# A linear-attention and gated-convolution kernel: nine tokens of a head on a partition, and K and Q transposed by DMA

## The chip, the cores and the metric

The kernel runs on one core of one Trainium2 chip. A core has a matrix engine (TensorE, "PE" in the profile, its weight loads "PEld"), three engines for elementwise work (VectorE "DVE", ScalarE "ACT", GpSimd "POOL"), a queue that only issues DMAs (SyncE, "SP") and 16 DMA engines. TensorE reads SBUF, the on-chip memory of 128 partitions, and writes PSUM, here eight banks of 128 x 512 fp32 values. Each engine runs its own instructions in order and waits for others by semaphores. The metric is the device time of one execution in microseconds, less is better.

## The reference

There are 8 batches of 8 heads, 576 tokens, head size 64, and 128 features. The first half is linear attention, and its output, heads side by side (512 wide), goes through a gated causal convolution:

```python
def phi(x):
    proj = np.einsum('bhsd,df->bhsf', x, w_phi)
    proj = proj - np.max(np.abs(proj), axis=-1, keepdims=True)
    return np.concatenate([np.exp(proj), np.exp(-proj)], axis=-1)
q_p, k_p = (phi(q), phi(k))
kv = np.einsum('bhsf,bhsd->bhfd', k_p, v)
z = np.sum(k_p, axis=2)
num = np.einsum('bhsf,bhfd->bhsd', q_p, kv)
den = np.einsum('bhsf,bhf->bhs', q_p, z)[..., None] + 1e-06
x = num / den                       # heads side by side: (8, 576, 512)

for k in range(5):                  # xp: x with four zero rows ahead
    gate_pre += conv_w[k][None, None, :] * xp[:, k:k + S, :]
gate = 1.0 / (1.0 + np.exp(-gate_pre))
out = gate * (x @ w_val) @ w_out
```

The inputs and the output are fp32; the kernel multiplies in bf16.

## The kernel before

**Tiling of the attention.** The first 512 tokens of a head lie four consecutive ones to a partition on 128 partitions (`main_src`, line 179: `j=4`). The last 64 tokens of the heads are the "tails": those of two batches share 128 partitions, 64 rows each. A *unit* is 1024 rows of K and of Q, eight blocks of 128 rows by 64 values: a main unit is a pair of heads, a tail unit the tails of all 16 heads of two batches. So there are 32 main and 4 tail units, numbered 0 to 35, a tail unit first in each group of nine.

Each unit goes through the same steps. `T` (line 331): eight TensorE transposes of 128x128, two blocks each, four of K and four of Q, into one PSUM bank. `Tc`: one copy to the SBUF tile `T`, by DVE (`D`) or ScalarE (`A`). `PK` and `PQA` (line 342): projections of K and Q with tokens on partitions, 16 matmuls each that use 64 rows of the array, two row halves in turn. `mKa`, `mK`, `mQa`, `mQ` (line 356): the largest absolute value of a row, on DVE. `K0` to `K3` (line 388): exponentials of K's projection, on ScalarE. `E` (line 382): exponentials of the row maximum, which go onto V rather than K. `V` (line 408): V times that factor, mostly on POOL, with the factor itself as a 65th column so that the sum `z` comes along. `PQ` and `SH` (lines 466, 476): Q's projection with features on partitions, and the subtraction of its row maximum by matmuls with a negated identity. `Qa`, `Q` (line 484): its exponentials.

`KV` (lines 445, 450): for a head pair, 16 matmuls with the main blocks and 4 with the tails, 65 columns each; the tails' V tile (`VZ`) is zero in the other batch's rows, so the contraction runs over all 128. `KVM`: the copy to SBUF. `NUM`: 16 matmuls per main unit (line 509), and per tail unit 32 that use half of the array's columns (line 523). `XN` (lines 534, 536): reciprocal and multiplication. `XP` (lines 545, 548): a DMA transpose of the result, issued by SP, into `XT` (main) or `XH` (tails).

**The second half.** `GA` (line 604): the convolution as matmuls with diagonal 64x64 weights, on the four quarters of the array, per batch in two ops. The tokens of a partition differ by their offset j = 0 to 3, so a tap is a shift of j, and where it crosses the four a shift by one partition. `VAa`, `VAb` (line 617): x times `w_val`. `TH`: tanh for the gate. `GV` (line 633): gate times value. `OUT` (line 642): times `w_out`; `OE` the copy out with a factor 0.5, `ST` the store by SP. `GAt`, `THt`, `GVt`, `OUTt`, `OEt` and `STt` do the same for the tails, and `HL` copies the four tokens ahead of a tail.

**What sets the order.** The string `ORDER` (lines 32 to 101) lists every step in turn, with PSUM banks after `@` and the engine after `:`. Each engine gets its instructions in that order, and the DMAs their queue: loads of fp32 inputs, cast to bf16 on the way, are issued by POOL (`LD`, line 295; V of batch 0 by SP, uncast), transposes and stores by SP. Tile pools give the buffers: five of `T`, three of `VT`, thirteen of `KVS`.

Of the kernel before, what the change touches and what calls it, by code (L numbers as in the profile page):

```python
# [42 lines left out]
SH7 mQa8 LD15 mK8 K08 K37 PQA9@2,3 mQ8 mQa9 KV5@7 KVM5:D mQ9 T10@5 Tc10:D K18 PQ8@0,2 SH8 Qa7
PK9@4,7 mKa9 T11@3 E7 V7:P Q7 PK10@5,6 Tc11:D K28 mKa10 LD14 DG0:P Qa8 K38 KV6@3 Q8 K09 NUM5@0 mK9
KVM6:D NUM6@2 XN5 K010 mK10 KV7@0 K29 K110 XN6 K19 KVM7:D T12@5 PK11@1,4 mKa11 K210 HL0:P Tc12:D
XP6 LD16 K39 GA0@2 K310 mK11 K011 NUM7@6 VAa1@0 LD40 XN7 E8 VAb1 TH0 GV1 V8:P PK12@2,5 PQA10@3,6
K111 PQ9@1,7 SH9 VAa2@0 K211 mQa10 mKa12 LD19 VAa0@3 mK12 E9 LD17 K311 Qa9 VAb0 mQ10 KV8@4 KVM8:D
VAb2 GV0 PQA11@1,6 K012 V9:P Q9 mQa11 K212 PQ10@4,7 SH10 mQ11 K112 T13@3 Tc13:D NUM8@1 XN8 E10
K312 Qa10 Q10 GA1@5 TH1 PK13@3,4 mKa13 NUM0@1 V10:P KV10@7 XN0 KVM10:D XP5 XP0 XP8 E11 E12 K013
mK13 VAa3@5 GV2 PQ11@6,1 SH11 K113 Qa11 V11:P VAb3 GV3 LD18 K213 NUM10@2 XN10 T14@0 Tc14:D Q11  # L50
KV11@7 XP7 PQA12@5,6 K313 GA2@2 E13 TH2 PK14@0,1 mQa12 mQ12 PQA14@4,5 OUT1@6 OE1:A KVM11:D
PQA13@7,2 mQa14 V12:P V13:P mKa14 LD34 K014 mQ14 mQa13 K114 PQ12@3,4 SH12 XP10 KV12@6 mQ13 T15@5
Qa12 KVM12:A Tc15:D OUT2@7 Q12 mK14 K214 NUM11@2 E14 PQ13@0,6 SH13 Qa13 XN11 XP11 NUM12@4 OE2:D
XN12 T16@2 VAa6@3 PK15@7,0 mKa15 GA3@4 mK15 K314 V14:P VAa4@1 Q13 Tc16:D VAb4 K015 TH3 PQA15@6,2
GV4 K215 K315 PQ14@5,4 SH14 mQa15 K115 mQ15 VAa5@1 VAb5 PK16@0,6 Qa14 VAb6 Q14 KV13@7 GV5 mKa16
mK16 Vb9:P K016 VAa7@2 T17@1 GV6 E15 V15:P Tc17:D LD33 KVM13:A KV14@5 LD22 HL1:P NUM13@3 K116 K216
PQ15@0,7 KVM14:A VAb7 XN13 K316 SH15 GV7 PK17@1,3 mKa17 Qa15 K017 Q15 K117 LD35 mK17 XP13
PQA16@5,6 mQa16 OUT3@4 XP12 K217 OE3:D mQ16 OUT0@2 OUT5@0 K317 OE5:A E16 V16:P OE0:D NUM14@4 T18@1
XN14 Tc18:D GAt0@6 THt0 ST1 GVt0 E17 PQ16@2,3 PK18@1,0 SH16 Qa16 mKa18 Q16 T19@4 Tc19:D GA4@5 TH4
PQA18@7,2 mK18 mQa18 E18 KV15@4 KVM15:D K018 LD38 K118 V17:P K218 OUT6@3 mQ18 OE6:D PQA17@7,6 K318  # L60
mQa17 mQ17 LD20 GA5@4 TH5 PK19@2,3 mKa19 PQ18@1,7 SH18 K019 KV16@0 mK19 Qa18 KVM16:D K119 E19
NUM15@5 VAa9@4 VAb9 LD21 V19:P K219 ST3 XN15 XP15 GV9 NUM16@0 XN16 Q18 LD24 T20@2 VAa8@5 XP16 VAb8
K319 T21@6 PQA19@4,0 PQ17@1,7 Tc20:D PK20@2,3 Tc21:A SH17 GV8 Qa17 mQa19 VAa10@5 VAb10 mKa20 K020
XP14 KV17@6 V18:P mQ19 Q17 GV10 VAa11@0 PK21@1,4 KVM17:D K120 mK20 mKa21 mK21 K220 VAb11 GV11
NUM17@5 XN17 OUTt0@2 K021 K221 LD26 KV19@7 OUT7@0 K320 OEt0:D OE7:D K121 T22@3 PQA20@5,2 mQa20
PQ19@1,6 mQ20 SH19 KVM19:A K321 Tc22:A HL2:A PK22@0,5 mKa22 NUM9@3 XN9 XP9 Qa19 OUT4@7 Q19 K022
E20 mK22 Vb18:P PQA21@2,1 mQa21 XP17 OE4:D K122 K222 T23@6 K322 V20:P E21 NUM19@3 XN19 XP19 E22
PQ20@2,0 V21:P SH20 Qa20 mQ21 OUT9@7 OE9:D LD23 PQA22@5,4 mQa22 Tc23:D Q20 LD36 mQ22 PQ21@3,1 SH21
KV20@7 KVM20:A LD25 Qa21 V22:P T24@2 PQA23@6,0 mQa23 PK23@5,7 mKa23 Q21 OUT8@4 OE8:A K023 OUT10@3
mK23 E23 V23:P OUT11@6 Tc24:D OE10:D NUM20@1 K223 K323 K123 XN20 XP20 OE11:A GA6@3 PK24@1,2  # L70
PQ22@7,5 SH22 ST5 T25@6 TH6 mKa24 mK24 Tc25:D Qa22 Q22 E24 K024 KV21@3 KVM21:D KV22@4 GA7@6
KVM22:D HL3:D mQ23 NUM21@4 TH7 VAa14@3 XN21 XP21 VAb14 K124 NUM22@6 LD37 K224 PQA24@1,5 GV14
PQ23@0,4 SH23 K324 Qa23 XN22 PK25@3,6 Q23 mQa24 mKa25 K025 KV23@7 T26@2 Tc26:A V24:P VAa15@1
KVM23:D VAb15 mQ24 ST7 K125 NUM23@4 mK25 K225 VAa12@0 VAb12 GV15 XN23 PK26@2,1 PQ24@7,3 K325
PQA25@4,5 mKa26 K026 E25 mQa25 SH24 Qa24 GV12 VAa13@6 mQ25 VAb13 T27@4 KV24@0 mK26 K126 Q24 XP23
PQ25@5,7 SH25 GV13 Tc27:D T28@2 Qa25 Q25 E26 KVM24:D Tc28:D XP22 PQA26@6,3 mQa26 mQ26 OUT13@4
V25:P V26:P K226 PK27@0,2 mKa27 LD28 OE13:A GAt1@5 mK27 KV25@7 K326 THt1 GVt1 K027 NUM24@3 K127
E27 K227 Vb27:P KVM25:D XN24 KV26@1 PK28@5,6 mKa28 XP24 LD27 K327 PQ26@7,0 SH26 mK28 Qa26 NUM25@3
XN25 HL4:A OUTt1@2 Q26 K028 K128 KVM26:D OUT14@7 OE14:D XP25 K228 PQA27@3,4 mQa27 mQ27 GA8@0 TH8
VAa16@7 VAb16 K328 OEt1:A NUM26@4 XN26 T29@3 Tc29:A NUM18@0 XN18 XP18 E28 OUT12@6 V28:P PK29@3,2  # L80
GV16 OE12:A PQ27@5,4 mKa29 PQA28@0,1 mQa28 mQ28 K029 SH27 Qa27 GA9@6 TH9 T30@0 ST11 VAa18@1 mK29
VAb18 Tc30:D PK30@0,5 GV18 V27:P OUT15@6 VAa17@7 VAb17 mKa30 Q27 OE15:D mK30 K129 E29 PQA29@4,6
V29:P mQa29 GV17 mQ29 PQ28@1,3 K229 K030 K130 SH28 T31@0 Tc31:D K230 VAa19@4 VAb19 Qa28 KV28@7 ST9
XP26 K329 PQA30@6,1 PQ29@2,0 SH29 GV19 mQa30 mQ30 Q28 KVM28:A K330 NUM28@3 XN28 PQ30@7,6 Qa29 E30
V30:P PK31@5,1 mKa31 SH30 PQA31@4,3 Q29 Qa30 mQa31 mK31 E31 mQ31 KV29@2 V31:P K031 K231 T32@0
OUT17@4 Tc32:D K131 OUT16@7 Q30 PK32@0,3 KVM29:D OE17:D KV30@2 mKa32 K331 OE16:A NUM29@4 KVM30:D
K032 T33@6 XP28 mK32 XN29 XP29 GA10@1 LD29 K132 Tc33:D PQA32@4,5 K232 K332 E32 PQ31@7,0 mQa32
HL5:P TH10 mQ32 OUT19@6 OE19:A NUM30@3 XN30 XP30 KV31@5 KVM31:A SH31 Qa31 Q31 PQA33@1,6 PK33@2,3
ST15 mKa33 mQa33 mQ33 GA11@4 VAa20@7 TH11 VAb20 VAa22@1 mK33 V32:P VAb22 T34@6 PQ32@4,5 K033 SH32
E33 GV22 Tc34:D NUM31@0 VAa21@6 VAb21 GV20 K133 XN31 V33:P PK34@2,7 K233 K333 mKa34 Qa32 Q32 mK34  # L90
XP31 PQ33@3,4 K034 K134 T35@0 STt1 KV32@1 KVM32:D OUT18@5 NUM32@1 K234 K334 ST13 SH33 GV21 VAa23@6
VAb23 OE18:A Tc35:D PK35@7,0 XN32 XP32 Qa33 Q33 GV23 mKa35 PQA34@5,1 mQa34 mQ34 K035 GAt2@2 THt2
VAa26@6 E34 mK35 GVt2 ST17 V34:P VAb26 K135 KV33@4 PQA35@5,1 E35 mQa35 PQ34@7,2 SH34 VAa27@3 K235
K335 Qa34 mQ35 Q34 VAb27 STt0 KVM33:D PQ35@1,0 GA13@4 TH13 V35:D GV26 SH35 OUT20@7 KV34@2 Qa35
OE20:A KVM34:A VAa25@4 Q35 OUT21@5 NUM33@1 XN33 NUM34@6 KV35@0 VAb25 XP33 XN34 OE21:A KVM35:A
VAa24@5 OUT22@2 HL6:D XP34 OE22:D ST19 NUM35@0 VAb24 XN35 GA12@6 XP35 TH12 GV24 GA14@0 GV25 ST21
OUT23@2 GV27 VAa29@6 TH14 VAb29 HL7:D VAa31@7 VAb31 OUTt2@4 GV29 VAa28@3 NUM27@0 XN27 XP27 GA15@5
OEt2:A VAa30@4 OUT26@0 OUT27@1 OE26:D TH15 OUT24@6 OE24:D OUT25@5 VAb28 VAb30 STt2 GV31 OE23:A
OE27:D GAt3@6 GV30 GV28 OE25:A THt3 GVt3 OUT29@5 OUT28@0 ST23 OE29:A OUTt3@7 OE28:A OUT31@0
OUT30@1 OEt3:A ST27 ST25 ST29 OE31:A ST28 STt3 ST31 OE30:D ST30  # L100
"""


class _U:
    pass

@with_exitstack
def kernel(  # L110
# [653 lines left out]
```

## Time and profile before

| | before |
|---|---|
| time, median of 3 runs | 233.53 us (233.13 to 233.78) |
| profiled execution | 234.24 us, of it span 232.5 us |
| mean granted TensorE clock | 0.972 |
| busy: TensorE, ScalarE, DVE, POOL | 205.8, 188.6, 184.2, 125.4 us |
| HBM read, written | 30.48 MB, 9.44 MB |
| DMA packets | 62002, of them 33420 under 512 bytes |

The span is the time from the first to the last instruction of the program on the core; the profiled execution has 1.74 us around it. The busy time of an engine is the union of its instructions' times; those of TensorE are pipelined, so that a matmul of 200 ns can start 30 ns after the one before it. What a group of matmuls costs is therefore read from one group's start to the next one's. In rows of the profile `x16` is a count, `128x65` partitions by elements, and `64*128` the rows and columns of the array that are used. Brackets or a last column tell how long the engine sat idle before, and what ended it.

### The profile page before, as it was taken

To read this page: it belongs to the slowest core of one execution; us is meant where nothing else is said; L and a number is where in the kernel's file an instruction comes from. 1 tells how busy PE (TensorE), PEld (TensorE's weight loads), DVE (VectorE), ACT (ScalarE), POOL (GpSimd) and SP (SyncE) were. 2 spreads that over 40 slices of the span, in tenths; PEclk is the share of its full clock that TensorE was granted. 3 is DMA by queue.
4 is the path that set the end of the run, shared out by engine and by line. 5 is a ranking of instruction groups with operands and counts; after the bars stand their busy time and mean duration, and the time that the engine had idled before them with its cause. 6 is when DMAs were issued, how large, how long until landed. Compare 5 with 4: busy or idle time off the path is not lost.

```text
span 232.5 us, 8372 instructions
## 1 busy us (share of the span) xinstructions
PE 205.8 (89%) x3497; PEld 139.5 (60%) x3516; DVE 184.2 (79%) x335; ACT 188.6 (81%) x419; POOL 125.4 (54%) x142
## 2 busy tenths in 40 slices
PE   1286797888999989899999999999899999999991
PEld 1264675666666746567666766766476667564550
DVE  5559669999989979699999879897799788554451
ACT  3189869999997988599999979998899999934251
POOL 8909935999979437774919751564526241100000
PEclk9998579999999999999999999999999999999997
DMA  8997995979999942999994992499903928126195
GB/s 151 246 198 97 106 180 80 92 101 178 129 194 128 139 32 32 129 257 177 128 114 68 180 186 92 39 115 126 214 6 37 169 77 259 38 52 200 27 355 185
DMA packets 62002, 30.90 MB, mean 133 GB/s; under 512 B 33420, under 2 KB 59148, under 8 KB 61964
## 3 DMA queue, kind: packets, MB, share of 16 engines
q0 software_dynamic: 36144, 14.29, 58.2%
q1 hardware_dynamic: 25468, 15.78, 33.6%
q8 instruction: 27, 0.44, 0.8%
q10 hardware_dynamic: 352, 0.30, 0.4%
q14 instruction: 11, 0.09, 0.2%
HBM read 30.48 MB, written 9.44 MB: 172 GB/s over the span
## 4 chain that ended last, share of the span: by engine, by line
PE 69%; ACT 11%; DMA 9%; DVE 5%; issue 3%; SPq 1%; POOL 1%; POOLq 0%; DVEq 0%; ACTq 0%
PE PS L617 11%; PE PS L642 10%; PE PS L342 7%; PE PS L604 7%; PE PS L476 7%; PE PS L445 6%; PE PS L331 6%; DMA XT<-XN 6%; PE PS L509 5%; ACT QTIL L484 5%; ACT KTIL L388 3%; DMA kT<-in_k_dram 3%; PE PS L466 3%; PE PS L681 2%; DVE MQ L356 2%
## 5 line engine op out<-in xcount | busy, mean ns | idle before, releaser
L408 POOL TENSOR_TENSOR VT<-vN,E 128x1024 bf16<-128x1024 bf16 x27 | 51.5, 1907 | 60.4 <-issue 34.2
L388 ACT ACTIVATE KTIL<-PS 128x512 bf16<-128x512 f32 x128 | 76.7, 666 | 5.3 <-DVE MK L356 5.1
L484 ACT ACTIVATE QTIL<-PS 128x512 bf16<-128x512 f32 x128 | 71.0, 666 | 2.5 <-PE PS L476 1.1
L356 DVE TENSOR_REDUCE MK<-PS 128x4 f32<-128x512 f32 x72 | 47.9, 683 | 7.5 <-PE PS L342 7.2
L356 DVE TENSOR_REDUCE MQ<-PS 128x4 bf16<-128x512 f32 x72 | 47.4, 683 | 1.3 <-PE PS L342 1.2
L342 PE MATMUL PS<-W,T 64*128 64x128 bf16 x576 | 29.6, 227 | 5.8 <-DVE T L224 1.9
L617 PE MATMUL PS<-XT,WVAL 128*128 128x512 bf16 x128 | 33.8, 380 | 0.3 <-DMA XT<-XN 0.3
L342 PEld LDWEIGHTS <-T 64*128 64x128 bf16 x576 | 18.3, 98 | 21.8 <-issue 11.9
L642 PE MATMUL PS<-WOUT,GV 128*128 128x512 bf16 x111 | 29.9, 380 | 1.2 <-issue 0.5
L633 DVE SCALAR_TENSOR_TENSOR GV<-GATE,PS 128x512 bf16<-128x512 bf16 x32 | 21.6, 681 | 5.9 <-ACT GATE L612 3.1
L445 PE MATMUL PS<-VT,KTIL 128*128 128x65 bf16 x512 | 25.4, 198 | 0.8 <-DVE T L224 0.6
L536 DVE TENSOR_TENSOR XN<-PS,RCP 128x512 bf16<-128x512 f32 x36 | 24.9, 691 | 1.2
L445 PEld LDWEIGHTS <-KTIL 128*128 128x128 bf16 x512 | 22.8, 100 | 3.7 <-DVE T L224 0.8
L476 PE MATMUL PS<-nident,MQ 128*128 128x128 bf16 x288 | 23.9, 229 | 0.5 <-issue 0.5
L612 ACT ACTIVATE GATE<-PS 128x1024 bf16<-128x1024 f32 x16 | 16.7, 1044 | 8.8 <-PE PS L604 8.7
L476 PEld LDWEIGHTS <-MQ 128*128 128x128 bf16 x288 | 17.6, 102 | 9.5 <-issue 8.8
L224 DVE COPY T<-PS 128x1024 bf16<-128x1024 bf16 x31 | 21.1, 684 | 2.7 <-PE PS L331 2.3
L509 PEld LDWEIGHTS <-QTIL 128*128 128x128 bf16 x512 | 19.3, 99 | 5.5 <-DVE KVS L224 1.1
L509 PE MATMUL PS<-KVS,QTIL 128*128 128x65 bf16 x512 | 21.4, 196 | 1.3 <-DVE KVS L224 0.8
L450 PE MATMUL PS<-VZ,KTt 128*128 128x65 bf16 x128 | 21.9, 196 | 0.0
L604 PE MATMUL PS<-XT,DIAG 64*64 64x384 bf16 (+3 forms) x512 | 20.6, 299 | 1.0 <-issue 0.8
L642 PEld LDWEIGHTS <-GV 128*128 128x128 bf16 x128 | 11.3, 98 | 12.4 <-issue 0.6
(73 smaller groups left out, 304.1 us busy)
## 6 DMA issues: line engine op xcount, KB each, us to landing
out_dram<-OS SPq DMA_DIRECT2D x14, 512.0 KB, 3.8
kN<-in_k_dram POOLq DMA_DIRECT2D x7, 512.0 KB, 9.0
qN<-in_q_dram POOLq DMA_DIRECT2D x7, 512.0 KB, 8.4
vN<-in_v_dram POOLq DMA_DIRECT2D x7, 512.0 KB, 6.9
vF<-in_v_dram SPq DMA_DIRECT2D x2, 512.0 KB, 7.6
out_dram<-OSt SPq DMA_DIRECT2D x8, 128.0 KB, 2.4
out_dram<-OS SPq DMA_DIRECT2D x4, 256.0 KB, 2.9
qT<-in_q_dram POOLq DMA_DIRECT2D x8, 64.0 KB, 5.2
```

The source lines that it names most:

```text
L342: nc.tensor.matmul(PS[:, bank[rg], blk * P:(blk + 1) * P], u.T[r, i, blk, :], W2[r, :], start=True, stop=True,)
L356: nc.vector.tensor_reduce(dst, PS[:, bank, :].rearrange("p (b f) -> p b f", f=F), AX.X, ALU.max, apply_absolute_value=True,)
L388: nc.scalar.activation(u.KT[:, ft, rg, :, :].rearrange("p b f -> p (b f)"), PS[:, u.PK[rg], :], AF.Exp, scale=1.0 if ft == 0 else -1.0,)
L408: eng.tensor_tensor(dst[:, :, :, 0:D], x.unsqueeze(1).to_broadcast([n, 2, 8, D]), e.unsqueeze(3).to_broadcast([n, 2, 8, D]), ALU.mult,)
L445: nc.tensor.matmul(o, u.KT[:, ft, rg, h2 * 2 + j2, :], u.VT[:, ft, (h2 * 2 + j2) * 2 + rg, :], start=(c == 0), stop=False,)
L476: nc.tensor.matmul(PS[:, u.PQ[rg], blk * P:(blk + 1) * P], u.MQ[:, rg, blk:blk + 1].to_broadcast([P, P]), nident[:, :], start=False, stop= ...
L484: nc.scalar.activation(u.QT[:, ft, rg, :, :].rearrange("p b t -> p (b t)"), PS[:, u.PQ[rg], :], AF.Exp, scale=1.0 if ft == 0 else -1.0,)
L509: nc.tensor.matmul(ps[:, j2, x * E1:(x + 1) * E1], u.QT[:, ft, rg, h2 * 2 + j2, :], u.KVS[:, (ft * 2 + h2) * E1:(ft * 2 + h2 + 1) * E1], s ...
L536: nc.vector.tensor_tensor(u.XN[:, :, :, :], nv[:, :, :, 0:D], RCP[:, :, :].unsqueeze(3).to_broadcast([P, 2, 4, D]), ALU.mult,)
L604: nc.tensor.matmul(ps[c, par, j0 * P:j1 * P], DIAG[r, dt, 4 - dl, :], mv, start=(i == 0), stop=(i == len(parts) - 1), skip_group_check=True,)
L617: nc.tensor.matmul(PS[:, m.val[jt], :], WVAL[:, dt, jt * P:(jt + 1) * P], XTs[m.b % 2][:, dt, :, 16:PL], start=(dt == 0), stop=(dt == 3),)
L642: nc.tensor.matmul(PS[:, bank[0], :], m.GV[:, jt, j * P:(j + 1) * P], WOUT[:, jt, :], start=(jt == 0), stop=(jt == 3),)
```

## The change

The tokens of a pair of heads, 2 x 576 = 1152, now lie nine consecutive ones to a partition: the first head on partitions 0 to 63, the second on 64 to 127. There are no tails. A pair has nine blocks, two batches have 72, and a unit is eight blocks in a row, whatever pair they are of: again 36 units. Loads bring 2304 consecutive bytes of source to a partition, into six tiles that live through the whole kernel, and all of them are issued by POOL.

Because a block now holds two heads, KV sums over 64 rows at a time: per pair, feature half and block, two matmuls, one on each row half of the array, into two banks. A *quad* is two pairs (four heads); its KV is done in two ops (`KVa`, `KVb`), 1152 matmuls in all, and its copies are `CA`, `CB`. NUM is done in three ops of 24 matmuls a quad, each with 64 weight columns, in pairs that write the two partition halves: a low and a high token offset side by side. XN follows in three steps of 6 x 64 values. Eight of the nine blocks of a quad go to `XT` by two DMA transposes, the ninth (token offset 4) by one TensorE transpose (`XQ`) and a copy (`XD`).

GA keeps its 2560 columns per quarter, in 15 matmuls a quarter instead of 8, since the two halves of a partition range take their neighbours from different places. The 64 tokens with offset 4 of two batches take the place of the tails in `GAt` and the steps after it. A store of the main part is split in two, by partition halves.

From unit 10 on, T and Tc are replaced by two DMA transposes straight into the tile `T`, issued by SP: `TK` for K and `TQ` for Q. `T` has six buffers instead of five, `VT` four instead of three, `KVS` four of twice the size, and the order string is new throughout.

```diff
     def op_T(i, bank):
         u = units[i]
         u.Tps = PS[:, bank[0], :].bitcast(BF16).rearrange("p (i b t) -> p i b t", i=2, b=4)
         for n, name in enumerate(("k", "q")):
             for blk in range(4):
-                nc.tensor.transpose(u.Tps[:, n, blk, :], col(u, name, blk), ident_bf[:, :])
+                nc.tensor.transpose(
+                    u.Tps[:, n, blk, :], unit_cols(u, name)[:, blk * P:(blk + 1) * P], ident_bf[:, :],
+                )
+
+    def xbar(i, n):
+        u = units[i]
+        if not hasattr(u, "T"):
+            u.T = ktp.tile([P, 2, 4, P], BF16, name="T")
+        nc.sync.dma_start_transpose(u.T[:, n, :, :], unit_cols(u, "kq"[n]))
...
+    def kv(m, ab):
+
         for ft in range(2):
-            for h2 in range(2):
-                o = u.KVps[:, (ft * 2 + h2) * E1:(ft * 2 + h2 + 1) * E1]
-                for c in range(4):
-                    j2, rg = c // 2, c % 2
+            for j in range(NJ):
+                u, rg, blk, c = place(m, ab, j)
+                for h2 in range(2):
+                    r = slice(h2 * 64, h2 * 64 + 64)
+                    o = (ab * 2 + ft) * E1
                     nc.tensor.matmul(
-                        o, u.KT[:, ft, rg, h2 * 2 + j2, :],
-                        u.VT[:, ft, (h2 * 2 + j2) * 2 + rg, :],
-                        start=(c == 0), stop=False,
+                        PS[:, m.kv[h2], o:o + E1], u.KT[r, ft, rg, blk, :], u.VT[r, ft, c, :],
+                        start=(j == 0), stop=(j == NJ - 1),
                     )
-                nc.tensor.matmul(
-                    o, ut.KT[:, ft, h2, u.hp, :],
-                    VZ[u.G % 2][u.b % 2][:, ft, 2 * u.hp + h2, :],
-                    start=False, stop=True,
-                )
...
+    BLOCKS = [[(ab, 5 + i), (ab, i)] for ab in range(2) for i in range(4)] + [[(0, 4), (1, 4)]]
+
+    def op_NUM(n, bank):
+        m, s = quads[n // 3], n % 3
+        m.num[s] = bank[0]
+        for x3 in range(3):
+            for h2 in range(2):
                 for ft in range(2):
-                    for bb in range(2):
-                        r = slice(bb * ST, (bb + 1) * ST)
+                    for c, (ab, j) in enumerate(BLOCKS[3 * s + x3]):
+                        u, rg, blk, _ = place(m, ab, j)
+
+                        o = (2 * x3 + (h2 ^ ab)) * E1
                         nc.tensor.matmul(
-                            ps[r, x // 4, (x % 4) * E1:(x % 4 + 1) * E1],
-                            u.QT[:, ft, h2, hp, r],
-                            pair_of[2 * u.G + bb, hp].KVS[:, (ft * 2 + h2) * E1:(ft * 2 + h2 + 1) * E1],
+                            PS[c * 64:c * 64 + 64, bank[0], o:o + E1],
+                            u.QT[:, ft, rg, blk, h2 * 64:h2 * 64 + 64],
+                            m.KVS[:, h2, (ab * 2 + ft) * E1:(ab * 2 + ft + 1) * E1],
                             start=(ft == 0), stop=(ft == 1), skip_group_check=True,
                         )
...
+    def op_XQ(n, bank):
+        m = quads[n]
+        m.XQ = PS[:, bank[0], 0:64].bitcast(BF16)
+        nc.tensor.transpose(m.XQ, m.XN[:, 8, :], ident_bf[:, :])
...
+        parts = [(0, None, 0, 4, None)]
+        for dl in range(1, 5):
+            parts.append((dl, 0, dl - 1, 4, lambda p, dt, dl=dl: high(p, dt, -1, 4 - dl)))
+            if dl > 1:
+                parts.append((dl, 0, 0, dl - 1, lambda p, dt, dl=dl: low(p, dt, 5 - dl, 4)))
             if dl < 4:
-                parts.append((dl, dl, 4))
-            if dl > 0:
-                parts.append((dl, 0, dl))
+                parts.append((dl, 1, dl, 4, lambda p, dt, dl=dl: low(p, dt, 0, 4 - dl)))
+            parts.append((dl, 1, 0, dl, lambda p, dt, dl=dl: high(p, dt, 4 - dl, 4, 1)))
```

A stretch of the order around the first units that are transposed by DMA (`TK10`, `TQ10`), and the one around `LD21`, the load of K of batch 6:

```diff
+mKa8 T9@5 PQA8@7,2 Tc9:D mQa8 mK8 NUM6@5 TK10 Qa6 PQ7@1,7 K27 K08 DG0:P K37 XQ1@4 Q6 SH7 TQ10 K18
...
+PQA24@5,4 NUM28@0 V23:P XN28 mQa24 Q23 LD21 NUM29@2 mK24 mQ24 K024 TK26 XN29 XP17 OUT13@3 XP19
+OE13:A K124 E24 V24:P XQ8@0 XD8:D TQ26 GAt1@5 PQ24@4,3 K224 K324 SH24 XQ9@2 THt1 XD9:A GVt1
+OUT12@0 OUT14@7 Qa24 Q24 PK25@5,6 OE12:D mKa25 PK26@0,4 mK25 GA8@1 OE14:A KVa10@3,7 KVb10 XP18
+mKa26 mK26 K025 CA10:D CB10:D TH8 K125 K225 PQA25@1,2 mQa25 mQ25 K026 OUT15@5 NUM30@7 XN30 K325
+TK27 K126 NUM32@3 K226 PK27@1,0 mKa27 PQ25@6,2 SH25 NUM31@7 XN32 XN31 OE15:A E25 VAa17@5 VAb17
+mK27 PQA26@3,7 mQa26 V25:P K326 E26 V26:P TQ27 ST11 K027 Qa25 OUTt1@4 K127 mQ26 TK28 PK28@3,6
```

## The prediction

> **What bounds the kernel now.** I read the busy shares first, then the same by stretches of the span, then who waited for whom, and last the order of TensorE's work in time, which gives the prices.
>
> ```profile
> PE 205.8 (89%) x3497; PEld 139.5 (60%) x3516; DVE 184.2 (79%) x335; ACT 188.6 (81%) x419; POOL 125.4 (54%) x142
> ```
>
> ```profile
> core 0: us, PE busy (x) PEld busy (x) DVE busy (x) ACT busy (x) POOL busy (x), PEclk, DMA share, GB/s
> 24.00:56.00 32.00, 27.88 (x486) 21.43 (x482) 27.80 (x53) 29.25 (x70) 25.24 (x30) 0.88 1.12 123
> 56.00:95.00 39.00, 36.91 (x659) 24.45 (x658) 34.95 (x63) 35.68 (x84) 27.73 (x31) 1.00 1.28 112
> 125.00:165.00 40.00, 38.60 (x720) 26.43 (x720) 33.98 (x64) 36.13 (x78) 22.91 (x25) 1.00 0.88 121
> 165.00:205.00 40.00, 39.74 (x694) 26.93 (x699) 33.37 (x61) 38.23 (x87) 13.52 (x14) 1.00 0.52 111
> ```
>
> From 56 to 205 us TensorE is 97% busy (144.2 of 149 us) at full clock: there it is the bound. ScalarE is close behind it, 38.2 of 40 us in the last of these stretches. Before 56 us all engines take turns and the granted clock is 0.88. The 16 DMA engines are full until 125 us (share over 1) and half idle after 165.
>
> **Prices.** TensorE runs on without gaps here, so what a group costs is the time from its start to the next group's:
>
> ```profile
> 120.47 0.40 PE L331 MATMUL PS<-ident_bf,kN 128*128 128x128 bf16 x4
> 120.70 0.39 PE L331 MATMUL PS<-ident_bf,qN 128*128 128x128 bf16 x4
> 120.93 0.65 PE L509 MATMUL PS<-KVS,QTIL 128*128 128x65 bf16 x16
> ...
> 160.21 0.40 PE L342 MATMUL PS<-W,T 64*128 64x128 bf16 x8
> 160.44 0.38 PE L466 MATMUL PS<-T,W 64*128 64x512 bf16 x2
> 160.66 0.39 PE L342 MATMUL PS<-W,T 64*128 64x128 bf16 x8
> 160.98 0.34 PE L476 MATMUL PS<-nident,MQ 128*128 128x128 bf16 x3
> ```
>
> A unit's eight transposes take 0.46 us. Eight 64-row matmuls take 0.22 to 0.23 us when the next group is tiled alike, and 0.32 us when the next takes the whole array (160.66 to 160.98): a change of tiling costs about 0.095 us. Eight 64-row matmuls of 128 columns in 0.225 us are 56 ns a pair, where one whole-array matmul of 128 columns takes 57 ns (0.46 over 8): two row halves run at once.
>
> ```profile
> 66.12 0.70 PE L523 MATMUL PS<-KVS,QTt 128*64 128x65 bf16 x32
> 66.75 0.30 PE L445 MATMUL PS<-VT,KTIL 128*128 128x65 bf16 x4
> ...
> 125.50 0.10 PEld L342 LDWEIGHTS <-T 64*128 64x128 bf16 x2
> ```
>
> Thirty-two column-half matmuls (64 outputs, 65 columns) take 0.63 us with one change of tiling: 33 ns a pair, about the 31 ns of one whole-array matmul of 65 columns (a KV op's 20 go from 124.33 to 124.96). The last line, a look that ends at 125.51, shows two 64-row weight loads begun within 10 ns: loads to the two halves do not queue either.
>
> **The change on TensorE.**
> - Units 10 to 35 get K and Q transposed by DMA: 26 x 0.46 = -12.0 us. The ninth block of each quad needs one transpose instead (XQ): 16 x 0.057 = +0.9.
> - KV: 32 ops of 20 matmuls, 0.63 us each, are 20.2 us. After: 1152 matmuls with 64 rows, 65 columns. No row shows that form. Lower end: pairs at 31 ns, 576 x 0.031 = 17.9; upper end: no overlap, 35.7. I take 33 ns a pair as for the column halves, 19.0: the 64-row pairs of the projections and their paired loads stand nearest. So -1.2 us (ends -2.3 and +15.5).
> - NUM: 512 whole matmuls at 31 ns and four tail ops at 0.53 are 18.0 us; after, 576 column pairs at 33 ns are 19.0: +1.0.
> - The convolution GA: the same 2560 columns a quarter, in 15 rounds instead of 8. One op takes 1.22 us (99.59 to 100.81); GAt's 40 matmuls take 0.70 (96.35 to 97.05) for 10 rounds of 128 columns. Less 0.1 each for the tiling change, the two give 0.417 ns a column and 6.7 ns a round. So 7 x 6.7 ns x 16 = +0.8 us (if a 64-column round cost what a 128-column one does, 60 ns, about +2.5).
> - Changes of tiling, counted in the two instruction orders: 165 before, 198 after: 33 x 0.095 = +3.1 us.
>
> Sum: -12.0 + 0.9 - 1.2 + 1.0 + 0.8 + 3.1 = -7.4 us on the engine that bounds.
>
> **The other engines, costed at nothing while TensorE covers them.** DVE loses 22 T copies (684 ns) and two memsets, and gains 12 reciprocals with smaller divisions, 11 XD copies and five output copies: about -8 of 184 us. ScalarE loses four T copies (1033 ns) and five output copies (some 630 ns), gains two KVS copies (427 ns) and five XD: about -5 of 188.6. POOL loses the eight tail scalings (1905 ns and 251 ns): -17. If TensorE shrinks more than ScalarE, ScalarE is late next.
>
> **SP and the DMA engines.** SP gets 52 more transposes, and loses the eight of the tails.
>
> ```profile
> L545 SPq DMA_TRANSPOSE XT<-XN x32: 1189/1210/2460, 28.4 to 208.9; - x32
> ...
> DMA to landing us min/median/max: 2.5/4.6/10.4
> ```
>
> 84 transposes at the median 1.21 us are 102 us; 44 stores at about 0.55 are 24. That is 126 us, nearly all after 45 us (72 of the 288 input transposes are done by then, nine units), in an in-order queue that also waits for XN and OS. What stands behind such a wait is now the T of a later unit, so PK and PQA, the row maxima and ScalarE's exponentials wait with it. Six T buffers let SP run ahead. Loads get longer runs (2304 bytes of a source row instead of 1024), the 24 tail load DMAs go, and V of batch 0 moves from SP to POOL's queue, which issues two more such loads (0.94 us each) where it issued 22 tail DMAs (about 0.7). Landing between 2.5 us (quiet, after 189 us) and 10.4 (under loads): with a unit's TensorE work at about 5.2 us (188 over 36), a T issued two units ahead is safe at either end, one issued one unit ahead only at the median. The last K load (LD21) stands behind POOL's scaling of unit 23, so T27 and T28 have least room. I put 2 us on such waits (ends 0 and about 15).
>
> **The start.** TensorE idles 3.5 us until 11.25 us, for the tails' K and Q, POOL's first four DMAs (landed by 11.1). Afterwards the second unit needs POOL's first two, of larger size, and SP's loads of V no longer run beside them. Between nothing and -2.5 us; I take -1.
>
> The profiled execution took 234.24 us (span 232.5 and 1.74 around it); the median is 233.53. 233.53 - 7.4 + 2 - 1 = 227.1; I say 227.
>
> **The rivals.**
> 1. *The crossbar sets the pace (slower).* Issues of 2 to 2.46 us occur where two transposes follow each other or loads run. At a mean of 2.0, 84 x 2.0 + 24 = 192 us from about 45 us on ends at 237 and a last landing, so 239. It decides from a mean of 1.9. For it: the long issues, landings of 8 to 10 us around 70 us, orders from different sources in one queue. Against: the median of 1.21, fewer bytes in flight late. The Trainium skill speaks for it too: VectorE: DVE Perf Modes, under "Rules for kernel authors", sends a 128x128 transpose to TensorE where PSUM will do and to the crossbar otherwise; the trace's 0.23 us for four blocks against 1.21 us of issue agrees in direction.
> 2. *Weight loads do not overlap (slower).* KV at one load per 31 ns: 35.7 instead of 19.0, so 227 + 16.7 = 244. Against: the two loads begun within 10 ns. The Trainium skill (TensorE: Matmul & The Clock Gate, "LDWEIGHTS") says that a load's time goes by columns, whatever the rows; the trace agrees for single loads (98 ns with 64 rows, 100 with 128), and by that rule alone, loads in a queue, 244 would come out.
> 3. *ScalarE paces the middle.* Then only its 5 us and the start show, and waits for T eat part: 229 to 231.
> 4. *All that is freed counts.* 16 of TensorE's 27 idle us lie before 56 us; a third of these gone, and no waits for T: 219 to 221.
>
> **How the numbers follow.** The forecast with its spread of waits (222 to 231) has 0.45, rival 3 0.10, rival 4 0.08, waits for T that eat just the gain 0.05, rival 1 0.27, rival 2 0.05. Faster by over 0.3% (what a measurement of this kernel can tell) is 0.63, within it 0.05, slower 0.32. The range to 241 leaves out rival 2 and the worst of 1, the low end 218 some of 4.
>
> **What would show it.** Right: TensorE's busy time near 199 us, KV's 72 matmuls of a quad in about 1.2 us, idle TensorE before PK or PQA under 3 us after 56 us. Wrong: waits of PK or PQA for DMA T over 9 us in sum; SP's transposes over 1.9 us each; KV at 2 us a quad; ScalarE at over 97% in the middle; a clock under 1.00 there, which would say that waits throttle TensorE.

## The result and the profile after

The changed kernel takes 257.26 us (median of 4 runs, 253.92 to 260.84), the kernel before beside it 233.45: ratio 1.093, 95% interval 1.083 to 1.103. The forecast was 227 us, range 218 to 241, chance of slower 0.32. It was wrong, in sign and by 30 us.

The profiled execution took 258.07 us, span 256.3. Executions of this kernel spread by 2.7%, and the ratios and intervals in this document leave out the slower, disturbed ones (the profiled ones of this kernel and of run 14 are such), so that the loss to explain is 9.3%, or 21.7 us. The page after: busy times, and the DMA queues with packets, MB and share of 16 engines (q0 POOL's loads, q1 SP's transposes and stores, q8 TensorE's code, as is shown below):

```profile
PE 209.3 (82%) x4796; PEld 137.8 (54%) x4796; DVE 176.2 (69%) x346; ACT 186.0 (73%) x415; POOL 97.7 (38%) x109
...
q1 hardware_dynamic: 49500, 20.80, 48.3%
q0 software_dynamic: 13552, 14.91, 40.3%
q8 instruction: 37, 0.61, 1.0%
```

The same queues before:

```profile
q0 software_dynamic: 36144, 14.29, 58.2%
q1 hardware_dynamic: 25468, 15.78, 33.6%
q8 instruction: 27, 0.44, 0.8%
```

DVE, ScalarE and POOL lost work as forecast (184.2 to 176.2, 188.6 to 186.0, 125.4 to 97.7 us), and TensorE stands idle for 47.0 of the span instead of 26.7. Two things grew: the packets of q1, and TensorE's instructions (matmuls and weight loads) from 7013 to 9592, with the pieces of code from 27 to 37. By stretches of the span, after:

```profile
core 0: us, PE busy (x) PEld busy (x) DVE busy (x) ACT busy (x) POOL busy (x), PEclk, DMA share, GB/s
24.00:56.00 32.00, 24.89 (x694) 19.19 (x688) 23.39 (x53) 25.67 (x58) 20.97 (x23) 0.88 0.92 144
56.00:95.00 39.00, 33.12 (x747) 20.04 (x748) 29.51 (x56) 31.33 (x72) 12.99 (x14) 0.96 1.07 154
125.00:165.00 40.00, 33.75 (x811) 21.81 (x811) 28.96 (x58) 32.12 (x74) 16.52 (x17) 0.96 1.10 156
165.00:205.00 40.00, 31.68 (x724) 20.66 (x725) 25.89 (x50) 28.66 (x69) 13.64 (x14) 0.88 0.98 140
```

From 56 to 205 us TensorE is now busy for 127.2 us instead of 144.2 of 149; ScalarE fell with it (38.2 to 28.7 us in the last stretch), and the DMA share stays near 1 to 205 us, where it was 0.52 in the last stretch. No engine is busy throughout any more. What TensorE waited for (us, times, longest), after:

```profile
PE PS L481 <- issue: 10.0, 4, 4.0
...
PE PS L411 <- issue: 4.6, 5, 2.4
PE PS L314 <- DMA T<-kN: 3.4, 2, 2.4
PE PS L411 <- POOL VT L388: 3.4, 1, 3.4
PE PS L573 <- DMA XT<-XN: 2.8, 1, 2.8
PE PS L586 <- DMA XT<-XN: 1.7, 1, 1.7
```

The largest, 15.4 us in sum with one more row of 0.8, is "issue": nothing that the profile shows as awaited. It falls on the lines with many small matmuls (L481 NUM, L411 KV), in the middle of an op. In the order of time, after:

```profile
37.55 1.45 PE L411 MATMUL PS<-VT,KTIL 64*128 64x65 bf16 x72
38.93 0.28 PE L481 MATMUL PS<-KVS,QTIL 128*64 128x65 bf16 x5
43.18 0.71 PE L481 MATMUL PS<-KVS,QTIL 128*64 128x65 bf16 x19 [3.97 <-issue]
```

A NUM op stops after 5 of its 24 matmuls for 4 us, with all operands there. The records of q8 explain it. My working from the trace (us; "issued" counts TensorE's matmuls and weight loads, k numbers the pieces of 16 KB):

```
kernel         stop    resume  issued  piece k landed  issued - 256k
after          39.21   43.18   1213    3       41.88   445
after          58.04   60.91   1979    6       59.55   443
after          92.19   94.59   3259    11      93.10   443
after         137.54  139.89   5307    19     137.92   443
```

Each stop begins at the same count, and ends 1.3 to 2.0 us after the piece lands: TensorE has run out of its own code. So it is at every such stop of over 1 us in the runs below (counts 429 to 445). The first two stops, at 35.1 us (0.8 us) and at 39.2 us (the longest), lie before SP issues the first transpose of K, at 47.36 us.

By the trace, the span can be split in three: work (busy time weighted with the granted clock), what the lower clock adds to it, and idle time. Before, 232.5 us are 201.4 + 4.4 + 26.7; after, 256.3 us are 195.2 + 14.1 + 47.0. So TensorE has 6.2 us less to do, loses 9.7 us more to the lower clock, and stands idle for 20.3 us more. This is an account and not yet a cause.

### The profile page after: what moved, and what is told of

The parts are those of the page before. It is cut to its first block, busy times and chain, and to the rows that moved or that the text cites. A ratio compares the mean times of both kernels' runs of the same rounds, so it can differ in the third digit from the quotient of the medians.

```text
span 256.3 us, 10969 instructions
## 1 busy us (share of the span) xinstructions
PE 209.3 (82%) x4796; PEld 137.8 (54%) x4796; DVE 176.2 (69%) x346; ACT 186.0 (73%) x415; POOL 97.7 (38%) x109
## 5 line engine op out<-in xcount | busy, mean ns | idle before, releaser
L383 POOL TENSOR_TENSOR VT<-vN,E 128x1024 bf16<-128x1024 bf16 x35 | 66.5, 1901 | 122.1 <-issue 71.3
L455 ACT ACTIVATE QTIL<-PS 128x512 bf16<-128x512 f32 x144 | 77.5, 633 | 17.5 <-PE PS L447 17.3
L314 PE MATMUL PS<-W,T 64*128 64x128 bf16 x576 | 30.6, 234 | 7.9 <-DMA T<-kN 3.4
L481 PE MATMUL PS<-KVS,QTIL 128*64 128x65 bf16 x1152 | 26.8, 201 | 10.8 <-issue 10.0
L481 PEld LDWEIGHTS <-QTIL 128*64 128x64 bf16 x1152 | 22.9, 115 | 17.8 <-issue 15.9
L411 PE MATMUL PS<-VT,KTIL 64*128 64x65 bf16 x1152 | 25.5, 198 | 7.9 <-issue 4.6
L314 PEld LDWEIGHTS <-T 64*128 64x128 bf16 x576 | 19.1, 101 | 21.1 <-issue 11.0
L411 PEld LDWEIGHTS <-KTIL 64*128 64x128 bf16 x1152 | 22.5, 100 | 11.3 <-issue 10.4
L495 DVE TENSOR_TENSOR XN<-PS,RCP 128x384 bf16<-128x384 f32 x48 | 26.7, 557 | 1.7
L573 PE MATMUL PS<-XT,DIAG 64*64 64x192 bf16 (+4 forms) x960 | 23.1, 245 | 2.9 <-DMA XT<-XN 2.8
L447 PE MATMUL PS<-nident,MQ 128*128 128x128 bf16 x288 | 23.9, 230 | 0.0
L573 PEld LDWEIGHTS <-DIAG 64*64 64x64 bf16 x960 | 16.9, 111 | 8.7 <-issue 6.9
L586 PEld LDWEIGHTS <-WVAL 128*128 128x128 bf16 x128 | 11.3, 101 | 13.8 <-issue 5.1
## 6 DMA issues: line engine op xcount, KB each, us to landing
vN<-in_v_dram POOLq DMA_DIRECT2D x2, 288.0 KB, 10.7
```

The lines of the kernel that those rows point to most:

```text
L314: nc.tensor.matmul(PS[:, bank[rg], blk * P:(blk + 1) * P], u.T[r, i, blk, :], W2[r, :], start=True, stop=True,)
L383: e.tensor_tensor(u.VT[:, :, :, 0:D], unit_cols(u, "v").rearrange("p (c d) -> p c d", d=D).unsqueeze(1).to_broadcast([P, 2, 8, D]), E.to_b ...
L411: nc.tensor.matmul(PS[:, m.kv[h2], o:o + E1], u.KT[r, ft, rg, blk, :], u.VT[r, ft, c, :], start=(j == 0), stop=(j == NJ - 1),)
L447: nc.tensor.matmul(PS[:, u.PQ[rg], blk * P:(blk + 1) * P], u.MQ[:, rg, blk:blk + 1].to_broadcast([P, P]), nident[:, :], start=False, stop= ...
L455: nc.scalar.activation(u.QT[:, ft, rg, :, :].rearrange("p b t -> p (b t)"), PS[:, u.PQ[rg], :], AF.Exp, scale=1.0 if ft == 0 else -1.0,)
L481: nc.tensor.matmul(PS[c * 64:c * 64 + 64, bank[0], o:o + E1], u.QT[:, ft, rg, blk, h2 * 64:h2 * 64 + 64], m.KVS[:, h2, (ab * 2 + ft) * E1: ...
```

## The experiments

**Theories.** S: the layout's half-array pairs need more code than arrives. C: the DMA transposes crowd the DMA engines, so that loads, XT, T and code all come late. Q: T is late by its place in SP's in-order queue. Ratios are to the kernel before on the same chip, with 95% intervals.

**1. T by TensorE on the new layout.** Units 10 to 35:

```diff
-K026 OUT15@5 NUM30@7 XN30 K325 TK27 K126 ... mQ26 TK28 PK28@3,6 mKa28 K227 TQ28
+K026 T28@1 OUT15@5 Tc28:D NUM30@7 XN30 K325 K126 ... mQ26 PK28@3,6 mKa28 K227
```

> The changed kernel with the crossbar undone: units 10 to 35 get K and Q transposed by TensorE and one DVE copy again, each at a bank that is free two to six us of TensorE work ahead of its PK; all else, the order of the other steps too, is the changed kernel's. Theory 'crossbar' (late T's, and the 52 transposes' traffic holding up everything else that goes by DMA, TensorE's instructions among it): the stalls go, and with 12 us more of TensorE work (26 x 0.46) it lands at 236 to 243 us. Theory 'instructions' (TensorE's code, 9602 loads and matmuls against 7035, comes in pieces of 256 by DMA, and the short matmuls of KV and NUM eat a piece in about 3 us, so that it runs dry whenever a piece is late, whoever fills the DMA engines): the stalls inside NUM and KV stay, and it lands at 250 to 262 us.

Measured: 271.06 us, 1.154 (1.144 to 1.164). It doesn't settle the question: the order has no free PSUM bank for T, and the added transposes wait for one, about 20 us, as in these rows:

```profile
PE PS L480 <- issue: 7.5, 4, 4.2
PE PS L288 <- DVE MQ L327: 5.9, 4, 2.0
```

What it does show is the first row: stops for code stay without any crossbar transposes of K and Q, 9.6 us in sum with two smaller rows, and the longest again at 38.6 us.

**2. The crossbar alone, on the old layout.**

```diff
-Tc27:D T28@2 Qa25 Q25 E26 KVM24:D Tc28:D XP22 PQA26@6,3
+VAa12@0 VAb12 GV15 XN23 TK28 TQ28 PK26@2,1 ... XP22 PQA26@6,3
```

> The kernel before with the crossbar alone: the 24 main units from unit 10 on get K and Q by two DMA transposes from SP, issued 9 us of TensorE work ahead of their PK, and lose their eight TensorE transposes and the copy; layout, KV, NUM and GA stay as before. Theory 'crossbar': 72 or more transposes in SP's queue bring late T's and late XT's, 234 to 246 us. Theory 'instructions': there are fewer instructions than before (6650) and no dense stretch, so the saving of 24 x 0.46 = 11 us of TensorE work shows but for small waits, 223 to 229 us.

Measured: 246.20 us, 1.050 (1.040 to 1.059), at the upper end of what theory C (here "crossbar") expected. Half of the loss comes with the transposes alone, although TensorE has, by the price of T, 11 us less to do (8.6 by the weighted busy time, 201.4 to 192.8).

**3. and 4. The changed kernel without late loads, and with half of NUM.**

```diff
     def op_LD(i):
         name, kind, n, p0, p1 = LOADS[i]
+        if kind == "m" and n >= 4:
+            return
```

> The changed kernel without the loads of K, Q and V of batches 4 to 7 (they compute on the values of batches 0 to 3 that the tiles still hold, so the output is wrong from batch 4 on); transposes and stores stay. If loads are what holds up TensorE's instructions and the T's: the idle TensorE time after about 95 us, some 20 us of the 34 in gaps, falls to under 6, and the time to 240 to 247 us. If the transposes among themselves do it: the gaps after 95 us stay, 252 us or more.

```diff
-                for ft in range(2):
+                for ft in range(1):
```

> The changed kernel with half of NUM: only the first of the two feature halves is multiplied (the numerators and denominators lack the other half), 576 matmuls and 576 weight loads fewer. TensorE loses 9.5 us of work (288 pairs at 33 ns). Theory 'instructions': the densest stretches are half as long and 1152 of 9602 instructions are gone, so the three stalls inside NUM (4.0, 2.9 and 2.4 us) go as well, and the clock that they cost: 236 to 244 us. Theory 'crossbar': the T's and the traffic are the same, the stalls move elsewhere, 247 to 252 us.

Measured, one run each: 245.30 and 247.83 us. The first time is in the range that late loads as the cause gave, but TensorE's idle time in gaps after 95 us only falls from 17.6 to 12.4 us, where under 6 was expected; the second is in the range of theory C (247 to 252). Either brings some 10 us and no more, since another wait takes over: idle before PK for T is 9.9 and 16.0 us instead of 3.4. Half of NUM is less work too, so its gain isn't one of waiting alone.

**5. and 6. The old layout without late loads, and with the crossbar on top.**

```diff
         name, kind, n, p0, p1 = LOADS[i]
+        if kind == "m" and n >= 4:
+            main[name, n] = main[name, 1 + (n - 1) % 3]
+            return
```

> The kernel before without its loads of K, Q and V of batches 4 to 7 (the units of these batches use the data of batches 1 to 3 again, so the output is that of other inputs). A control for the next run. Theory A (transposes by DMA lose only where they meet loads) and theory B (they lose wherever they stand) expect the same here: TensorE is 97% busy from 56 to 205 us with the loads, so little can be gained without them: 229 to 234 us.

> The kernel before, its units from 10 on (without tails) transposed by DMA, and no loads of K, Q and V of batches 4 to 7 (the data of batches 1 to 3 again). With the loads this crossbar variant took 246.2 us, 11.7 more than the kernel before. Theory A (the loss comes where transposes and loads share the 16 DMA engines): without the late loads the 24 x 0.46 = 11 us of TensorE come out in good part, 218 to 227 us, below the control without crossbar, and waits for T, XT and code pieces under 5 us in sum. Theory B (a transpose by DMA is itself too slow for this queue, or its landing too late): 238 to 246 us, and as long as with the loads the waits for T or XT stay.

Measured: 232.87 us, 0.998 (0.995 to 1.002), and 231.44 us, 0.990 (0.984 to 0.996). The transposes that cost 12 us beside the loads gain about 1 without them. Windows 95 to 125 and 125 to 165 us, first with loads (run 2), then without (run 6):

```profile
95.00:125.00 30.00, 23.52 (x401) 15.11 (x403) 23.02 (x41) 21.95 (x49) 16.53 (x21) 1.00 1.36 147
125.00:165.00 40.00, 34.50 (x607) 22.88 (x610) 29.11 (x53) 30.98 (x73) 22.07 (x25) 0.96 1.45 159
```

```profile
95.00:125.00 30.00, 28.12 (x514) 18.62 (x518) 26.65 (x49) 25.38 (x62) 16.25 (x17) 1.00 0.81 114
125.00:165.00 40.00, 39.09 (x690) 25.31 (x692) 33.19 (x63) 36.38 (x83) 19.80 (x21) 1.00 0.73 108
```

The DMA share is 1.4 and TensorE idles 12 of 70 us, or it is under 0.85 and TensorE idles 2.8. But even then most of the 11 us saved on TensorE is not gained; its busy time falls by 6.2 us (206.1 to 199.9), and its idle time grows by 4.9 us (24.4 to 29.3), about half of it before MQ, QTIL and XT. The range that was expected for run 6, 218 to 227 us, is missed.

**7. The changed kernel with whole-array KV and NUM.**

```diff
                 u, rg, blk, c = place(m, ab, j)
-                for h2 in range(2):
-                    r = slice(h2 * 64, h2 * 64 + 64)
-                    ...
-                        PS[:, m.kv[h2], o:o + E1], u.KT[r, ft, rg, blk, :], u.VT[r, ft, c, :],
+                o = (ab * 2 + ft) * E1
+                    PS[:, m.kv[j % 2], o:o + E1], u.KT[:, ft, rg, blk, :], u.VT[:, ft, c, :],
```

> The changed kernel with each pair of half-array matmuls of KV and NUM as one matmul of the whole array (31 ns instead of about 33 a pair): the work of TensorE is the same, but it has 1152 matmuls and 1152 weight loads less, 7298 instead of 9602, near the 7035 of the kernel before. KV then sums both heads of a block into one, so the output is wrong. Theory S (TensorE runs out of instructions: 37 pieces of code of 256 instructions come over a crowded DMA ring, where 27 came before): the idle time without a shown wait falls from 15.4 us to under 4, the clock rises, and the time falls to 236 to 243 us. Theory C (transposes and loads hold each other up, and code pieces are only one of the things that come late): the idle time moves to waits for T, XT or VT, and the time stays at 246 to 255 us.

Measured: 247.75 us, 1.049 (1.039 to 1.058). 28 pieces of code, and what TensorE waits for:

```profile
PE PS L314 <- DMA T<-kN: 10.0, 4, 3.0
PE PS L582 <- DMA XT<-XN: 3.5, 2, 2.6
...
PE PS L409 <- issue: 0.3, 1, 0.3
```

Code waits went from 15.4 to 0.3 us, as S said; but T and XT took over, and the time lies where C put it. How much of the 9.5 us is waiting stays open. By this case's prices about 5.5 are work (576 NUM pairs at 33 ns and 576 KV pairs at 36 against 31 ns: 4 us; 17 changes of tiling fewer, counted in the order, at 0.095: 1.6). The weighted busy time falls by only 1.1 us (195.2 to 194.1); plain busy time falls by 8.7 us (209.3 to 200.6), most of it because less of it lies under the lower clock (6.5 us lost to it instead of 14.1).

**8. The crossbar for the last eight units only**, on the old layout. Units 28 to 35 as in run 2, the others keep T:

```diff
-Tc27:D T28@2 Qa25 Q25 E26 KVM24:D Tc28:D XP22
+VAb12 GV15 XN23 TK28 TQ28 PK26@2,1 ... XP22
```

> The kernel before with only units 28 to 35 transposed by DMA, from about 165 us on, where the share of the DMA engines is 0.52 and the last loads are landing. Theory A (loss only beside loads): the 8 x 0.46 = 3.7 us of TensorE come out in part, 230 to 233 us. Theory B (loss wherever they stand): 234 to 238 us.

Measured: 232.45 us (11 runs) against 234.01, 0.992 (0.988 to 0.996): this version is faster than both kernels, than the one before by 0.8%. Its window in which the transposes run:

```profile
165.00:205.00 40.00, 38.80 (x661) 25.53 (x664) 31.28 (x57) 37.88 (x87) 13.65 (x14) 1.00 0.78 145
```

Here a transpose meets a DMA share of 0.5, lifts it to 0.78, and nobody waits.

**9. Halves without the crossbar**, on the old layout.

```diff
-                    nc.tensor.matmul(
-                        o, u.KT[:, ft, rg, h2 * 2 + j2, :],
...
+                    for f in range(2):
+                        r = slice(f * 64, f * 64 + 64)
+                        nc.tensor.matmul(
+                            o[r], w.KT[:, ft, rg, blk, r], x,
...
```

> The kernel before, each whole-array matmul of KV and of a main unit's NUM split into two of 64 output partitions (column halves, which run in pairs at 33 ns as against 31 ns for a whole one). The same result, no transposes of K and Q by DMA, but 1152 matmuls and 1152 weight loads more: 9339 TensorE instructions against 7035. Its own work: 1152 x 2 ns + 70 more changes of tiling (234 against 164, counted in the order) x 0.095 us = about +9 us at most, 240 to 243 us. Theory C (code pieces come late only because the transposes crowd the DMA rings) expects just that, and idle time with no wait shown under 4 us. Theory S (this many instructions outrun the supply of code by itself) expects idle time without a shown wait of 8 us and more, a clock below 0.95, and 247 to 256 us.

Measured: 244.77 us, 1.043 (1.032 to 1.053). 36 pieces of code:

```profile
PE PS L451 <- issue: 2.9, 2, 1.9
...
PE PS L525 <- issue: 1.8, 1, 1.8
```

All code waits are 5.5 us, against 2.2 before and 15.4 after. So both expectations miss in part: this many pieces are late now and then by themselves, but most of the 10 us here is work (busy 205.8 to 217.2). On the new layout pieces are later even without transposes of K and Q: 9.6 us in run 1, with stops of up to 4.2 us. Why they are later there is not shown.

**10. and 11. Whole-array, and T early; then without late loads too** (run 3's edit on top).

```diff
-K127 mQ26 TK28 PK28@3,6 mKa28 K227 TQ28
+K125 K225 TK27 TK28 PQA25@1,2 mQa25 mQ25 K026 TK29 OUT15@5 TQ28 ... PK28@3,6
```

> As the run with whole-array KV and NUM (247.75 us, output wrong as there), with the transposes TK and TQ moved forward in the order, to 10 us of TensorE's work ahead of their PK or PQA where the loads allow it (before: 0 to 12 us, units 27 to 29 under 1). There TensorE waited 11.2 us for T. Theory Q (T is late by its place in SP's in-order queue, behind transposes that wait for XN): the waits for T fall under 4 us and the time to 237 to 242 us. Theory C (the DMA engines are full, so something is late wherever it stands): waits for XT, T and others stay at 8 us and more in sum, 243 to 249 us.

> The run before this one, without the loads of K, Q and V of batches 4 to 7 too (data of batches 0 to 3 again): half-array pairs, late transposes and crowded DMA engines are all gone, the crossbar and the rest of the new layout stay. If these three are the whole loss, it comes out at the level of the old layout with crossbar and without late loads (231.4 us) or below it: 225 to 232 us. If the new layout has a cost of its own that is still unnamed (its convolution, its XQ and XD steps, its order), 235 us and more.

Measured: 240.47 us, 1.022 (1.008 to 1.035), and 229.40 us (226.28 to 234.10). In run 10 the waits for T fell from 11.2 to 4.9 us and the time by 7; but XT keeps 5.0 and code has 5.1 again, so Q is a part and C the rest. Run 11 is at the lower end of its expectation: with all three causes off, the changed kernel is below the kernel before without late loads (232.87) by some 3.5 us, or nearly 6 by its two faster executions: a rough size with four runs that spread by 3%. That is about half, or up to three quarters, of what it saves on TensorE.

**12. The crossbar from unit 19**, on the old layout.

```diff
-SH16 Qa16 mKa18 Q16 T19@4 Tc19:D GA4@5
+OE3:D mQ16 OUT0@2 TK19 TQ19 OUT5@0 ... SH16 Qa16 mKa18 Q16 GA4@5
```

> The kernel before with units 19 to 26 and 28 to 35 transposed by DMA (from about 105 us on), all loads kept. Between the runs with units 28 to 35 (ratio 0.992, DMA share 0.5 there) and 10 to 35 (ratio 1.050, DMA share over 1 there). If the loss is where the DMA engines are full (before: share 1.1 to 1.3 until 125 us, 0.88 until 165 us), units 19 to 26 lose what 28 to 35 gain or more: 233 to 240 us, idle before T or XT of 3 us and more between 100 and 165 us. If the loss is in the first units only (10 to 18, share over 1.2), it gains: 227 to 231 us.

Measured: 236.53 us, 1.009 (1.004 to 1.014). 8, 16 and 24 units give 0.992, 1.009 and 1.050: the more transposes and the earlier, the fuller the DMA engines that they meet (number and place change together here). The waits for T and XT are 2.7 us in the whole span, and a wait of 2.45 us for the load of a tail's K at 93.8 us is as large: the loss is small and spread.

**13. T early in the changed kernel itself** (the edit of run 10; half-array pairs stay).

> The changed kernel itself (half-array pairs, all loads, right output) with TK and TQ moved forward in the order to 10 us of TensorE's work ahead of PK and PQA where the loads allow it. With whole-array KV and NUM this move brought 7.3 us. Theory Q (place in the queue counts by itself): 248 to 253 us here as well. Theory S+C (late code is what TensorE meets first here: 15.4 us idle without a shown wait, but only 3.4 us for T): 254 to 259 us, and the idle time without a shown wait stays over 10 us.

Measured: 255.04 us, 1.085 (1.074 to 1.095). TensorE waits:

```profile
PE PS L480 <- issue: 14.9, 6, 5.5
...
PE PS L410 <- issue: 5.2, 3, 4.3
PE PS L313 <- issue: 2.9, 2, 2.5
PE PS L572 <- DMA XT<-XN: 2.5, 2, 2.2
```

No wait for T is left, and code waits rose from 15.4 to 23.2 us. The move that brought 7 us in run 10 brings no measurable gain here. The wait that was removed came back as waits for code.

**14. and 15. Transposes that nobody uses, and plain copies in their place.** The kernel before, complete, with 48 DMAs more (the last two lines are those of the two runs):

```diff
+        dst = vF[:, (2 * i + n) % 8, :].bitcast(BF16)
+        nc.sync.dma_start_transpose(dst.rearrange("p (b t) -> p b t", b=4), x)   # 14
+        nc.sync.dma_start(dst, x)                                                # 15
```

> The kernel before, unchanged, plus the 48 DMA transposes of K and Q of the main units from 10 on, issued by SP at the same places as in the crossbar variant (246.2 us), into space that is no longer used. Nobody waits for them, and TensorE still makes its own T. Theory C (they crowd the DMA engines and SP's queue, and everything else that comes by DMA is late): 242 to 258 us, DMA share over 1 until 165 us, TensorE idle for code pieces and XT. Theory T (what was lost was TensorE waiting for the T tiles themselves): 233 to 237 us.

> The same 48 DMAs with the same bytes (128 KB each) at the same places, as plain copies within SBUF instead of transposes. If the transposing is what crowds the DMA engines (a transpose of this size has 512 packets of 256 bytes), a copy is cheap: 233 to 237 us. If any DMA traffic of this size does it: as the run before, 240 us and more.

Measured: 246.15 us, 1.047 (1.037 to 1.057), and 238.31 us, 1.008 (1.002 to 1.014). This is the cleanest answer: nobody waits for these transposes, no engine but SP has anything more to do, and the loss is that of run 2. So the transposes cost 11 us on the old layout by what they do to others, without any wait for T. Run 2 saves work on TensorE and loses as much; waits for T (3.7 us there) are among what takes that saving. The same bytes as plain copies cost a sixth of it. One rival is not separated: SP's queue is longer too. Its issues take 157.7 us in run 14, 110.4 in run 15 and 78.6 before, and from the end of an XN to the issue of its transpose 3.1, 2.4 and 2.0 us pass in the mean. Windows of run 14, then of run 15:

```profile
95.00:125.00 30.00, 25.22 (x451) 17.19 (x451) 24.37 (x45) 24.00 (x52) 14.96 (x19) 1.00 1.38 146
125.00:165.00 40.00, 35.57 (x621) 24.54 (x621) 31.48 (x57) 31.68 (x73) 23.66 (x25) 0.96 1.26 157
```

```profile
95.00:125.00 30.00, 28.33 (x525) 19.45 (x525) 26.86 (x50) 26.76 (x64) 18.25 (x19) 1.00 1.36 198
125.00:165.00 40.00, 38.39 (x738) 26.98 (x740) 34.85 (x65) 35.52 (x79) 22.78 (x25) 1.00 1.04 156
```

At the same share, 1.36 to 1.38, the copies move 198 GB/s and the transposes 146. In run 14 the convolution then waits 5.7 us for an XT:

```profile
77.42 1.50 PE L617 MATMUL PS<-XT,DIAG 64*64 64x512 bf16 x20 [5.74 <-DMA XT<-XN]
```

The transposes of XN issued from 68 to 73 us landed after 10.1 to 10.7 us there (median before: 4.6). In that wait, from 72 to 76 us in slices of 0.1 us, the throughput of all DMA engines of run 14:

```profile
GB/s 187 179 184 179 187 182 187 179 189 177 187 182 184 338 172 185 164 179 166 179 161 164 151 118 20 21 8 8 13 8 15 108 174 200 195 182 190 177 177 177
```

It lies near 183 GB/s and breaks down for 0.7 us. The trace has the packets: those of transposes are 256 bytes in about 31 ns, those of loads 512 bytes in 59 ns, and of those begun from 74.2 to 75.1 us a tenth take 0.8 us or more. Such breaks are not special to this run. With ten or more packets in flight and under 40 GB/s for at least 0.3 us, I count 19 in run 14, 10 in run 15, 14 in the kernel before and 26 in the changed one; in 13 of the 14 before, packets of 256 bytes on q1, the size of the transposes', are in flight. Why they come, and what they cost, is not shown.

## Why the prediction was wrong

- **The sum on TensorE held roughly.** The 72 matmuls of KV take 1.38 us with the change of tiling (37.55 to 38.93), 36 ns a pair for my 33, which is +1.5 us over the kernel; GA's op went from 1.22 to 1.25 us, as worked out. Busy time is 209.3 us and not 199, but some 28 us of it lie under half the clock: if each busy microsecond is weighted with the granted clock (my working from the trace), the work falls from 201.4 to 195.2 us, -6.2 for my -7.4. Run 11 against run 5 has -8.1 us busy (197.9 against 206.1), with whole-array pairs.
- **The step that failed is the cost of SP's DMAs to the others.** I asked only how late T would land and put 2 us on it. The rows with a share over 1, and of 0.88 from 125 to 165 us, stood in my second fence, and I left out what 52 transposes do to everybody else on full engines. Run 14 measures that term on the old layout, with 48 transposes: about +11 us, with T taken out of the matter. In it q1 takes 134 us of all 16 engines (54.5% of the span) instead of 78 (33.6%): 56 us more (20 more with the copies of run 15), where the half-idle stretch from 165 to 205 us had room for 19 (0.48 of 40).
- **A resource was missing: TensorE's own code.** The sum counted the pairs by their time and not by their number. The page before has the 27 pieces and 7013 instructions, the order gave the count after; nothing in the prediction priced it. In the changed kernel these pieces are late by 15.4 us in sum (13.2 more than before). With whole-array pairs 0.3 us are left in run 7 and 5.1 in run 10. Without the transposes of K and Q it is 9.6 us on the new layout (run 1) and 5.5 on the old one (run 9), and 4.8 of the 15.4 us come before the first of them is issued. So both add to it, the half-array pairs more, and neither alone explains it.
- **"TensorE is the bound, so what it saves is saved"** held in no run. Even without late loads the crossbar gained 1.4 of 11 us (runs 5, 6).
- **Rival 1 had the sign but not the mechanism.** SP's transposes took 1.57 us in the mean of all 84 (by the trace), under the 1.9 from which its queue would set the pace, and the waits for T stayed at 3.4 us. The place in the queue does matter once code is not late (run 10). The rule of the Trainium skill cited there (VectorE: DVE Perf Modes, "Rules for kernel authors"), which sends a 128x128 transpose to TensorE where PSUM will do, was right in this case by more than the issue time, except late in the span: eight units of transposes from 165 us on gained 0.8% (run 8). The Trainium skill (Advanced Engine Details and Errata, "X-Bar Transpose (TRN2)") also says that transpose DMAs are as fast as regular ones; beside loads this case disagrees: 1.047 against 1.008 for the same bytes.
- **Rivals 2, 3 and 4 fell:** weight loads of the two row halves do overlap (KV at 36 ns a pair, not 62), ScalarE is 72% busy from 165 to 205 us, and idle time on TensorE grew.
- **Of the marks**, the clock was the one that spoke: 0.96, 1.00, 0.96 and 0.88 in the four stretches from 56 to 205 us. Whether it is a cause of its own stays open. After, two executions with a mean clock of 0.946 and 0.938 have spans of 252.1 and 254.7 us; but executions of the kernel before at 0.971 and at 0.998 have the same span, 231.9 us. No run changed the clock alone. Idle TensorE before L314 (PK and PQA) was 5.2 us after 56 us, not under 3; the marks for slow SP (1.9 us), KV (2 us) and ScalarE didn't show.
- **The start** gained about 2 us and lost them again: in the first 35 us TensorE is busy for 23.9 us against 22.0, in the first 56 us for 39.4 against 39.6, and the first two code stops (4.8 us) lie between.

What the loss of 9.3% (21.7 us) is made of, by ratios: 5.0% (about 12 us) comes with the transposes, net of what they save TensorE (run 2), and 4.4% (about 10 us) goes with the half-array pairs, by more work, late code and time under the lower clock in shares that are not settled (run 7). That the two fill the sum is partly luck, since the causes overlap, and the shares depend on the order in which they are removed.

## What to carry to other kernels

Price a DMA not only by when its own result lands, but by its time on the DMA engines in the stretch where it runs: where the share stood near 1 or above here, transposes made loads, other transposes and TensorE's code late (plain copies of the same bytes cost a sixth), and the wait appeared at whatever TensorE needed next. Moving work from a full engine to full DMA engines was no saving; eight units of transposes gained where they were half idle. And count instructions: two half-array matmuls that run in about the time of one whole (36 against 31 ns) still need twice the code.

## What was not expected of the hardware

- TensorE's code comes by DMA in pieces of 16 KB, one for about 260 matmuls and weight loads (7013 in 27, 7288 in 28, 9336 in 36, 9592 in 37). Late pieces show as idle "issue" in the middle of an op; every stop of over 1 us began 429 to 445 instructions beyond 256 times the number of the piece awaited, and ended 1.3 to 2.5 us after it landed.
- 48 transposes of 128 KB within SBUF beside loads cost 11 us of a kernel that doesn't use them; 48 plain copies of the same bytes 2.
- Throughput of all DMA engines falls to 10 to 40 GB/s for 0.3 us and more, with packets in flight, 14 times in the kernel before and 26 times in the changed one.
